# A two-layer decode kernel: the end of layer two rebuilt, one weight block fetched in row pairs, and a new order of loads and work

## The chip, the cores and the metric

The kernel runs on 1 core of one Trainium2 chip. The metric is the device time of one execution in microseconds (us); less is better. Profiles show one execution each, taken by the hardware profiler.

## What is computed

Four rows of 512 (one token each of four batches) pass an attention block and a gated block, twice, with the same weights and the same caches:

```python
def _A_ref(x, k_cache, v_cache, wq, wo):   # 32 query heads, 8 K/V heads of 128, 4096 positions
    q = (x @ wq), split into heads
    p = softmax(einsum(q, k) * Dh ** -0.5)
    return einsum(p, v), heads joined, @ wo
def _B_ref(x, w_gate, w_up, w_down):       # 512 -> 1792 -> 512
    return (sigmoid(x @ w_gate) * (x @ w_up)) @ w_down
x = x + _A_ref(_layernorm(x), k_cache, v_cache, wq, wo)
x = x + _B_ref(_layernorm(x), w_gate, w_up, w_down)
x = x + _A_ref(_layernorm(x), k_cache, v_cache, wq, wo)
x = x + _B_ref(_layernorm(x), w_gate, w_up, w_down)
```

## The kernel before

Attention is cut into 16 units, named by three digits: batch, half of the K/V heads (four heads, 16 query heads), layer. UNITS fixes their sequence; 301 is the last. A unit needs eight K tiles and eight V tiles of 512 KB (head s from 0 to 3, half q of the positions). They live in a ring of 24 slots. A tile of layer one that LOADS does not name again for layer two is kept in its slot until then: all of units 010, 110, 210 and 310, and two K tiles of 000. All weights have places of their own.

LOADS is the list of loads, issued by SP in this order. A word names kind, unit and piece: digits 0 to 3 are two single tiles, a to d both halves of one head as one DMA of 1 MB into two neighbouring slots, e to l one single tile. SP waits in order: a load whose slot is still in use holds all behind it. PAIRS names the blocks of w_o (eight heads, 1 MB each) that are fetched with two rows side by side, so that runs are twice as long; the merge of those heads then picks columns for even and odd rows apart.

A planner (`_Plan`) makes the program. Each operation is put with an engine, the keys that it reads and writes, an assumed cost and a rank, which comes from the place in LOADS of the data it needs, plus shifts (SHIFTS, by stage) and constants (CHAIN, PROJECT, KEPT_K and others). `schedule` replays all engines with assumed durations and takes the ready operation of least rank; this gives each engine's order, the slot of each tile, and fillers: constant matmuls (L1262) wherever PE would be idle. Some PSUM banks are locked by one user at a time (M, O, Q, P).

A unit runs as follows: DVE turns each K tile (L775); PE forms scores (L783), GROUPS[i] heads at a time; DVE and ACT form the exponentials (L807 to L842); PE multiplies with V (L874), two heads beside each other on column strips; ACT evicts (L903), PE merges into M (L916), DVE scales into oT (L938). The last unit's last pair of heads goes head by head, the second in bank G. `project` multiplies oT by a block of w_o into M (L1151) and adds it to x (L1162). In layer two it is called five times, the last two with four heads each. Then `last_chain` forms the row sums of x (L1183), the mean by a product with ones (L1187), x minus the mean twice (L1170, as fp32 xc and bf16 xT), squares (L1192), their sums (L1193), the mean square by small products (L1198), ACT's copy (L1203) and the power -1/2 on POOL (L1207). PE meanwhile runs gate and up products (L1027). The first up product in bank O waits for the power; ACT's sigmoid, DVE's product and transpose, w_down's products (L1098) and the output follow.

## Time and profile before

| | us |
|---|---|
| Median of 3 runs (lowest, highest) | 297.37 (297.33, 298.25) |
| The profiled execution | 298.3 |
| Its span, first to last instruction | 296.3 |
| Busy in the span: PE, DVE, ACT, POOL | 231.8, 171.0, 67.9, 10.9 |
| Mean granted TensorE clock | 0.983 of full |

In the page's rows L12 is line 12 of the program, PEld is PE's weight load, SPq the queue of the engine that issues the loads. Behind the bar of a group stand its busy time, the mean of one instruction in ns, and the idle time of the engine before them with what ended it. A row of a timeline begins with its start and its duration in us.

### The profile page before, as it was taken

The numbers are of one execution on the slowest core, as the hardware profiler recorded it, in microseconds if no ns is written. First come the engines' busy times: TensorE is split into PE (matmuls) and PEld (weight loads), VectorE is DVE, ScalarE is ACT, GpSimd is POOL, SyncE is SP. The second block draws the span as 40 slices with busy tenths as digits, with TensorE's granted clock in tenths as the row PEclk, the third lists the DMA queues.
The fourth block names the chain that finished last, engine by engine and source line by source line (L and its number), as shares of the span: only waits on it lengthen the run. The fifth ranks groups of instructions, "written<-read, shape, count | busy, mean of one in ns | idle before, by whom it ended". The sixth has DMA issues, their size and how long they took to land.

```text
span 296.3 us, 7884 instructions
## 1 busy us (share of the span) xinstructions
PE 231.8 (78%) x3440; PEld 112.4 (38%) x3440; DVE 171.0 (58%) x335; ACT 67.9 (23%) x179; POOL 10.9 (4%) x39
## 2 busy tenths in 40 slices
PE   1000684489988969998898889888997898997996
PEld 1000531144434424344464334454443354543443
DVE  4491277134351758995238878326889972388322
ACT  1000111110043210114442202323310234333512
POOL 7000000000000000000000000000000000000000
PEclk9999999779999989999999999999999999999999
DMA  7999999999999999999999999999999999999920
GB/s 279 428 424 421 421 395 395 422 420 390 390 418 374 369 421 409 413 410 420 404 385 410 411 412 416 408 401 357 385 414 409 409 408 407 406 405 410 406 106 3
DMA packets 28018, 114.03 MB, mean 385 GB/s; under 512 B 2768, under 2 KB 4816, under 8 KB 23504
## 3 DMA queue, kind: packets, MB, share of 16 engines
q1 hardware_dynamic: 27920, 113.52, 96.2%
q8 instruction: 27, 0.44, 0.6%
q14 instruction: 7, 0.06, 0.0%
q10 hardware_dynamic: 64, 0.01, 0.0%
HBM read 113.51 MB, written 0.00 MB: 383 GB/s over the span
## 4 chain that ended last, share of the span: by engine, by line
DMA 56%; PE 29%; DVE 7%; SPq 4%; issue 2%; ACT 1%; POOL 0%; ACTq 0%; DVEq 0%
DMA slots<-in_A_v_cache_dram 26%; DMA slots<-in_A_k_cache_dram 24%; PE S_ps L783 7%; PE PT_ps L1262 6%; DMA wd<-in_B_w_down_dram 6%; PE O_ps L874 5%; DVE slots L775 4%; SPq L581 4%; PE M_ps L963 2%; PE G_ps L1098 2%; PE G_ps L1027 1%; PE Q_ps L713 1%; PE U_ps L1027 1%; ACT pt_sb L842 1%; PE M_ps L916 1%
## 5 line engine op out<-in xcount | busy, mean ns | idle before, releaser
L775 DVE STREAM_TRANSPOSE slots<-slots 128x1024 int32<-128x1024 int32 x94 | 113.7, 1229 | 21.6 <-DMA slots<-in_A_k_cache_dram 20.4
L1262 PE MATMUL PT_ps<-wq 128*128 128x512 bf16 x308 | 82.9, 389 | 2.1 <-ACT pt_sb L842 2.1
L783 PE MATMUL S_ps<-slots,zq 128*32 128x512 bf16 x512 | 43.7, 406 | 7.2 <-DVE slots L775 3.4
L874 PE MATMUL O_ps<-slots,pt_sb 128*16 128x512 bf16 x504 | 37.9, 388 | 13.2 <-DMA slots<-in_A_v_cache_dram 7.7
L1262 PEld LDWEIGHTS PT_ps<-wq 128*128 128x128 bf16 x308 | 27.1, 100 | 34.6 <-issue 9.7
L783 PEld LDWEIGHTS S_ps<-slots,zq 128*32 128x32 bf16 x512 | 14.7, 97 | 27.5 <-DVE slots L775 8.6
L682 PE MATMUL Q_ps<-small,wq 128*128 128x4 bf16 x128 | 3.7, 166 | 24.6 <-DMA wq<-in_A_wq_dram 24.0
L903 ACT ACTIVATE slots<-O_ps 128x512 bf16<-128x512 f32 (+1 forms) x24 | 14.3, 595 | 37.2 <-PE O_ps L874 37.1
L821 ACT ACTIVATE p_sb<-S_ps,pt_sb 128x512 bf16<-128x512 f32 x16 | 13.3, 832 | 35.7 <-DVE pt_sb L814 31.5
L874 PEld LDWEIGHTS O_ps<-slots,pt_sb 128*16 128x16 bf16 x504 | 10.3, 88 | 28.0 <-issue 7.7
L842 ACT ACTIVATE pt_sb<-PT_ps 128x256 bf16<-128x256 f32 x32 | 10.8, 381 | 29.6 <-PE PT_ps L832 18.0
L963 PEld LDWEIGHTS M_ps<-oT,wo 128*128 128x128 bf16 x512 | 14.4, 96 | 6.1 <-DVE oT L942 1.7
L942 DVE TENSOR_TENSOR oT<-M_ps,real 64x8 bf16<-64x8 f32 x32 | 5.0, 155 | 20.2 <-PE M_ps L916 20.0
L963 PE MATMUL M_ps<-oT,wo 128*128 128x32 bf16 x512 | 15.8, 177 | 0.2
L748 DVE TENSOR_TENSOR zq<-Q_ps,real 128x256 bf16<-128x256 f32 x16 | 6.3, 395 | 16.3 <-ACT oT L692 10.5
L807 DVE TENSOR_REDUCE small<-S_ps 128x1 f32<-128x512 f32 x16 | 10.9, 683 | 5.8 <-PE S_ps L783 5.5
L1015 POOL TENSOR_TENSOR real<-real,small 128x1 f32<-128x1 f32 x8 | 4.4, 550 | 247.7 <-ACT real L1011 247.7
L682 PEld LDWEIGHTS Q_ps<-small,wq 128*128 128x128 bf16 x128 | 3.6, 104 | 24.8 <-DMA wq<-in_A_wq_dram 24.1
L916 PEld LDWEIGHTS M_ps<-small,slots 128*128 128x128 bf16 (+1 forms) x196 | 7.3, 107 | 11.8 <-ACT slots L903 6.1
L722 ACT ACTIVATE p_sb<-Q_ps 128x512 bf16<-128x512 f32 x8 | 4.8, 598 | 29.4 <-PE Q_ps L713 29.2
L916 PE MATMUL M_ps<-small,slots 128*64 128x4 bf16 (+2 forms) x196 | 9.5, 178 | 1.7 <-ACT slots L903 1.3
L713 PE MATMUL Q_ps<-wq,small 128*1 128x512 bf16 x128 | 9.8, 378 | 0.4 <-DVE small L989 0.3
(110 smaller groups left out, 174.5 us busy)
## 6 DMA issues: line engine op xcount, KB each, us to landing
slots<-in_A_k_cache_dram SPq DMA_DIRECT2D x66, 512.0 KB, 8.8
slots<-in_A_v_cache_dram SPq DMA_DIRECT2D x64, 512.0 KB, 10.4
slots<-in_A_v_cache_dram SPq DMA_DIRECT2D x16, 1024.0 KB, 14.9
slots<-in_A_k_cache_dram SPq DMA_DIRECT2D x14, 1024.0 KB, 13.5
wq<-in_A_wq_dram SPq DMA_DIRECT2D x2, 2048.0 KB, 17.6
wo<-in_A_wo_dram SPq DMA_DIRECT2D x4, 1024.0 KB, 16.8
wg<-in_B_w_gate_dram SPq DMA_DIRECT2D x1, 1792.0 KB, 16.8
wu<-in_B_w_up_dram SPq DMA_DIRECT2D x1, 1792.0 KB, 13.0
```

The source lines that it names most:

```text
L581: return e.dma_start(o, src)
L713: fns.append(lambda e, k=k, s=s: e.matmul(Q_ps[32 * s:32 * s + 1, :], lhsT=xT[:, b, k:k + 1], rhs=wq[:, k, hg * HC + s * 512:hg * HC + (s ...
L775: "dve", lambda e, t=t: e.transpose(ring[t.slot].bitcast(dt.int32), ring[t.slot].bitcast(dt.int32)),
L783: fns.append(lambda e, s=s, t=t, nn=nn, q=q: e.matmul(S_ps[qi][32 * s:32 * s + 32, :], lhsT=window(qi, s * NQ + nn, q), rhs=ring[t.slot].r ...
L807: dve(lambda e: e.tensor_reduce(ml[at], bank, AX.X, ALU.max, negate=True), [f"S{qi}s{s}" for s in ss], keys("ml", ss), 0.7)
L821: lambda e: e.activation(p_sb[at].rearrange("p (t j r) -> p t r j", j=32, r=2), bank.rearrange("p (t r j) -> p t r j", r=2, j=32), ACTF.Ex ...
L842: "act", lambda e, pr=pr: e.activation(pt_sb[:, (2 * i + pr) % 3], PT_ps[:, 256 * pr:256 * pr + 256], ACTF.Copy),
L874: fns.append(lambda e, m=m, at=at, v=v, c=c, q=q, pt=pt, o_ps=o_ps: e.matmul(o_ps[m:m + 16, :], lhsT=pt[:, at:at + 16], rhs=ring[v.slot][: ...
L903: lambda e, lent=lent, rows=rows, o_ps=o_ps, rows_of=rows_of: e.activation(ring[lent.slot][rows, 0:512], rows_of(o_ps[rows]), ACTF.Copy),
L916: return e.matmul(o, lhsT=turned[:, tt * P + at:tt * P + at + n], rhs=heads(tt), start=(tt == 0), stop=(tt == 3))
L963: fns.append(lambda e, k=k, n=n, h0=h0: e.matmul(M_ps[:, k * WIDE:(k + 1) * WIDE], lhsT=wo[:, h0 + n, k * P:(k + 1) * P], rhs=oT[:, b, h0 ...
L1262: S.filler(lambda e: e.matmul(PT_ps[:, 0:FILL], lhsT=wq[:, 0, 0:P], rhs=wq[:, 0, 0:FILL], start=True, stop=True), "PT")
```

## The change

The loads and the work are in a new order: LOADS, SHIFTS, GROUPS, LENT, the planner's constants and the assumed delays of loads are other values, and fillers are 256 columns wide, or 128 where 256 do not fit and no load is left to issue. Block 3 of w_o is fetched in row pairs too.

At layer two's end the last head's value products go in two parts, 288 columns to bank G and 224 to Q; ACT evicts the first and DVE the second. `last_part` takes the place of the last two `project` calls. The mean of x after the last block is not summed from x: the row sums of w_o's rows, made by DVE after the block's arrival and kept as two bf16 terms, are multiplied by oT onto the sum of the x before (`wo_mean`). The block's own product goes to bank S0, in two groups of four heads, and DVE forms `rest` (x minus mean) and then xc as one addition; ACT copies it to xT. The mean square is one product of ones by the squares and a masked sum on DVE (`bmask`) that also adds eps. The products of w_o are repeated over 64 columns instead of 32.

```diff
-DMA_DELAY = 0.979
-DMA_END = 1.047
-DMA_AGAIN = 2.392
+DMA_DELAY = 0.566
+DMA_END = 0.327
+DMA_AGAIN = 8.671
...
-PATIENCE = 2.164
+PATIENCE = 2.451
...
-LEAST = 4198
-WANTED = 35744
+LEAST = 13283
+WANTED = 154148
 FILL_FROM = 55.0
-FILL = 512
+FILL = 256
+SMALL = 128
+AMID = (2, 1)
...
-PAIRS = "02"
-GROUPS = "4244242442444444"
+PAIRS = "023"
+GROUPS = "2414222444442244"
...
-LENT = "K10021 V20001 V11100 V10130 V31101"
-CHAIN = 8.81
-PROJECT = 65.006
-KEPT_K = -26.257
-KEPT_V = 47.748
-REST_V = 60.815
...
-PUT_OFF = 69.06
+LENT = "V00020 V20001 K30001 V10101 V30110"
+CHAIN = 15.361
+PROJECT = -411.034
+KEPT_K = 2.445
+KEPT_V = 62.014
+REST_V = 286.312
...
+PUT_OFF = 365.25
 UNITS = "000 010 100 011 110 200 001 111 210 300 211 310 101 201 311 301"
-LOADS = "K010d wq1 K010a K000d K000c K000a V000c V000d wq0 V010b K000b K010b wo1 K100b K010c wg wo0 V000b V000a V010c K100a K1001 V010a wo2 V010d wo3 K1003 wu wd V1002 V1003 K2000 V100a K1103 K001l V100b K2001 K110b K110a K001g K1101 K2003 K2002 V110a K001k K001h K0012 V110b V1102 V1103 V200b V200a V0010 V0011 V2002 V2003 V001h K3001 K2103 V001l K3003 V001g K3000 K210a K2101 K210b V001k K3002 V210b V210a V2102 V2103 V3002 V3003 V3001 V3000 K3103 K201h K101f K101j K3101 K101h K101e K101i K1013 K201f K3100 K101g V3100 K3102 K2012 K201g K201e K201l K201k V3101 V101i V3103 V3102 V101e V101f V101j V1012 V101k V101l V201e V201i V201f K301l V201j K3011 K301e K301f K301i K301j V2012 K301k V2013 V301i V301f V301e V301j V301g V301k V301h V301l"
+LOADS = "V010b wq0 K100d K010a K000d wq1 V010d K0000 K0002 K000c K100c K010b K100b V0001 wo0 K100a wo1 K010c V010a V0000 K010d V010c wo2 wo3 V000c V000d wu wg wd V1002 V1003 K0013 K110b K2000 K110c K2002 V100a K110a V100b K2003 K110d K2001 K001i V110d V110b K001j K001h K001g V110a V110c V2000 V2001 V2002 V2003 V001j V001f V001e V001i K3000 K2101 V001k K210b V001l K300c K2103 K300d K210a V001h V001g K3002 V210a V210b V2102 V2103 V3002 V3003 V3000 V3001 K3103 K3101 K3100 K201k K101e V3101 K101h K101f K201g V3102 K3102 K101i K101g K201h K101j V3100 K2010 K1013 K201l V3103 K2012 V1010 V1011 V1012 V101k V101l K301j V201i V2010 V201j K301k K301f K301i K301h V2012 K301e K301g K301l V2013 V301a V301b V301g V301k V301h V301l"
...
+                if t + cost > at and not loads:
+                    op.fns, op.columns = [self.fill_small], 4 * SMALL
+                    cost = pe_cost(op, t)
...
+    FULL = 64
...
+    xc = spare[1][:, 0:16].rearrange("p (b k) -> p b k", b=B)
     sq = spare[0][:, 0:16].rearrange("p (b k) -> p b k", b=B)
-    xc = spare[1][:, 0:16].rearrange("p (b k) -> p b k", b=B)
+    rest = spare[0][:, 16:32].rearrange("p (b k) -> p b k", b=B)
+    bmask = spare[2][:, 0:B]
+    wo_mean = real[:, 68:76].bitcast(bf).rearrange("p (i n) -> p i n", i=2)
...
+    wo_sum = U_ps[:, FS:FS + 8]
...
-                                fns.append(lambda e, m=m, at=at, v=v, c=c, q=q, pt=pt, o_ps=o_ps: e.matmul(
-                                    o_ps[m:m + 16, :], lhsT=pt[:, at:at + 16], rhs=ring[v.slot][:, c * 512:(c + 1) * 512],
-                                    start=(q == 0 and c < 2), stop=(q == 1 and c >= 2),
-                                ))
+                                for bank, x0, x1 in ((G_ps, 0, 288), (Q_ps, 288, 512)) if alone else ((O_ps, 0, 512),):
+                                    fns.append(lambda e, m=m, at=at, v=v, c=c, q=q, pt=pt, bank=bank, x0=x0, x1=x1: e.matmul(
+                                        bank[m:m + 16, x0:x1], lhsT=pt[:, at:at + 16], rhs=ring[v.slot][:, c * 512 + x0:c * 512 + x1],
+                                        start=(q == 0 and c < 2), stop=(q == 1 and c >= 2),
+                                    ))
...
+                            "pe", fns, reads=[f"pt{part}", "Oz", "Gz", "Qz"], writes=["G", own("Q", first)] if alone else [own("O", first)],
+                            tiles=vs, rank=rank if len(some) == len(heads) else soon, columns=512 * 2 * len(vs), strips=2 * len(vs),
+                            lock=("Q" if alone else "O") if first else None,
...
+                cols = 288 if alone else 512
                 S.put(
                     "act",
...
+                    lambda e, lent=lent, rows=rows, o_ps=o_ps, rows_of=rows_of, cols=cols: e.activation(
+                        ring[lent.slot][rows, 0:cols], rows_of(o_ps[rows, 0:cols]), ACTF.Copy
...
-                    reads=["G" if alone else own("O")], writes=[lent.name], cost=0.6, rank=late, free=None if alone else "O",
+                    reads=["G" if alone else own("O")], writes=[lent.name], cost=0.17 + 0.43 * cols / 512, rank=late, free=None if alone else "O",
                 )
                 lent.users.append(S.ops[-1])
+                if alone:
+                    before = S.ops[-1].deps
+                    S.put(
+                        "dve",
+                        lambda e, lent=lent, rows=rows, cols=cols: e.tensor_copy(ring[lent.slot][rows, cols:512], Q_ps[rows, cols:512]),
+                        reads=[own("Q")], writes=["half"], cost=0.4, rank=late, free="Q",
+                    )
+                    for d in before:
+                        S._after(S.ops[-1], d)
+                    lent.users.append(S.ops[-1])
...
+                "pe", fns, reads=["sel_o"] + ([own("P")] if lent is None else ["half"] if alone else []), writes=[own("M", True)], cost=0.25, rank=late,
...
-            if k == 2:
+            if k == AMID[len(bs) > 1]:
                 amid()
...
+    def weight_sums(h0):
+
+        S.stage = "s"
+        for n in range(8):
+            S.put(
+                "dve", lambda e, n=n: e.tensor_reduce(wo_sum[:, n:n + 1], wo[:, h0 + n, :], AX.X, ALU.add),
+                reads=[f"wo{h0 // 8}"], writes=["U"], cost=0.6, rank=place[f"wo{h0 // 8}"] + 6.0,
+            )
+
+    def weight_means():
+
+        S.stage = "s"
+        rank = rank_v(seq[-1], 0)
+        S.put(
+            "dve", lambda e: e.tensor_scalar(wo_mean[:, 0], wo_sum, 1.0 / D, None, op0=ALU.mult),
+            reads=["U"], writes=["wo_mean0", "maskrs0", "maskrs1"], cost=0.16, rank=rank,
+        )
+        S.put(
+            "dve",
+            lambda e: e.scalar_tensor_tensor(
+                out=wo_mean[:, 1], in0=wo_sum, scalar=1.0 / D, in1=wo_mean[:, 0], op0=ALU.mult, op1=ALU.subtract
+            ),
+            reads=["U", "wo_mean0"], writes=["wo_mean1"], cost=0.16, rank=rank,
+        )
...
             cost=1.4, rank=-1e6,
         )
         S.put(
+            "dve", lambda e: e.tensor_reduce(bmask, ident.rearrange("p (m b) -> p b m", b=B), AX.X, ALU.add),
+            reads=["even"], writes=["pt2"], cost=0.3, rank=rank,
+        )
+        S.stage = f"z{h0}"
+        S.put(
             "dve", lambda e: e.tensor_reduce(xsum, x, AX.X, ALU.add),
             reads=[f"x{b}" for b in every_b], writes=[f"xsum{b}" for b in every_b], cost=0.2, rank=rank,
         )
         S.put(
-            "pe", lambda e: e.matmul(U_ps[:, 0:B], lhsT=ones, rhs=xsum, start=True, stop=True),
+            "pe", lambda e: e.matmul(U_ps[:, 0:B], lhsT=ones, rhs=xsum, start=True, stop=False),
             reads=["ones"] + [f"xsum{b}" for b in every_b], writes=["U"], cost=0.35, pairs=2, rank=rank,
         )
-        centre(xc, ["pt1"], rank)
-        centre(xT, [f"xT{b}" for b in every_b], rank)
-        S.put("dve", lambda e: e.tensor_tensor(sq, xc, xc, ALU.mult), reads=["pt1"], writes=["pt0"], cost=0.2, rank=rank)
-        S.put("dve", lambda e: e.tensor_reduce(xsq, sq, AX.X, ALU.add), reads=["pt0"], writes=[f"xsq{b}" for b in every_b], cost=0.2, rank=rank)
+        for g in range(2):
+            S.stage = f"z{h0 + 4 * g}"
+            heads = [f"oT{b}{h0 + 4 * g if (b, h0 // HG, 1) == seq[-1] else h0}" for b in every_b]
+            fns = []
+            for n in range(4 * g, 4 * g + 4):
+                for i in range(2):
+                    fns.append(lambda e, n=n, i=i: e.matmul(
+                        U_ps[:, 0:B], lhsT=wo_mean[:, i, n:n + 1].broadcast_to([P, P]), rhs=oT[:, :, h0 + n],
+                        start=False, stop=(n == 7 and i == 1),
+                    ))
+            S.put("pe", fns, reads=heads + ["wo_mean0", "wo_mean1"], writes=["U"], cost=0.0, rank=rank + 3.0 * g)
+            for k in range(KD):
+                fns = []
+                for n in range(4 * g, 4 * g + 4):
+                    fns.append(lambda e, k=k, n=n: e.matmul(
+                        S_ps[0][:, k * FULL:(k + 1) * FULL], lhsT=wo[:, h0 + n, k * P:(k + 1) * P],
+                        rhs=oT[:, :, h0 + n].unsqueeze(2).broadcast_to([P, B, FULL // B]),
+                        start=(n == 0 and k == 0), stop=(n == 7), skip_group_check=True,
+                    ))
+                S.put(
+                    "pe", fns, reads=heads + [f"wo{h0 // 8}"], writes=banks, rank=rank + 3.0 * g,
+                    columns=len(fns) * 4 * FULL,
+                )
+        rank = rank + 4.0
+        S.stage = "end"
+        S.put(
+            "dve", lambda e: e.tensor_tensor(rest, x, U_ps[:, 0:B].unsqueeze(2).broadcast_to([P, B, KD]), ALU.subtract),
+            reads=["U"] + [f"x{b}" for b in every_b], writes=["pt0"], cost=0.2, rank=rank,
+        )
+        moved = S_ps[0][:, 0:KD * FULL].rearrange("p (k b d) -> p b k d", k=KD, b=B)[:, :, :, 0]
+        S.put(
+            "dve", lambda e: e.tensor_tensor(xc, moved, rest, ALU.add), reads=banks + ["pt0"], writes=["pt1"], cost=0.2, rank=rank + 1.0,
+        )
+        S.put(
+            "act", lambda e: e.activation(xT, xc, ACTF.Copy),
+            reads=["pt1"], writes=[f"xT{b}" for b in every_b], cost=0.2, rank=rank + 1.0,
+        )
+        S.put(
+            "dve", lambda e: e.tensor_tensor(x, moved, x, ALU.add),
+            reads=banks + [f"x{b}" for b in every_b], writes=[f"x{b}" for b in every_b], cost=0.2, rank=rank + 9.0,
+        )
+
+    def last_chain(rank):
+
+        S.stage = "end"
+
+        S.put("dve", lambda e: e.tensor_tensor(sq, xc, xc, ALU.mult), reads=["pt1"], writes=["sq"], cost=0.2, rank=rank)
 
         def spread():
-            fns = []
-            for c in range(4):
-                fns.append(lambda e, c=c: e.matmul(Q_ps[32 * c:32 * c + B, 200:201], lhsT=xsq, rhs=mean1, start=True, stop=True))
             S.put(
-                "pe", fns, reads=["ones", "Qz"] + [f"xsq{b}" for b in every_b], writes=[own("Q", True)], cost=0.25, rank=rank, pairs=8, lock="Q",
+                "pe", lambda e: e.matmul(Q_ps[:, 200:216], lhsT=ones, rhs=spare[0][:, 0:16], start=True, stop=True),
+                reads=["ones", "Qz", "sq"], writes=[own("Q", True)], cost=0.3, rank=rank, pairs=2, lock="Q",
             )
             S.put(
-                "act", lambda e: e.activation(var[:, 0:1], Q_ps[:, 200:201], ACTF.Copy, bias=eps),
-                reads=[own("Q")], writes=["junk"], cost=0.2, rank=rank, free="Q",
+                "dve",
+                lambda e: e.scalar_tensor_tensor(
+                    out=sq, in0=Q_ps[:, 200:216].rearrange("p (b k) -> p b k", b=B), scalar=eps / KD,
+                    in1=bmask.unsqueeze(2).broadcast_to([P, B, KD]), op0=ALU.add, op1=ALU.mult, accum_out=var[:, 0:1],
+                ),
+                reads=[own("Q"), "pt2"], writes=["junk", "sq"], cost=0.27, rank=rank, free="Q",
             )
             S.put(
                 "pool", lambda e: e.tensor_tensor(rs_row, var[:, 0:1], mhalf, ALU.pow),
@@ -1240,6 +1332,8 @@
     passed = []
     first_q(0)
     queries(0, 0.0)
+    late = seq[-1][1] * HG
+    weight_sums(late + 8)
     for i, (b, hg, l) in enumerate(seq):
         passed.append(seq[i])
         if i == 1:
@@ -1252,14 +1346,20 @@
         if i and seq[i - 1][1:] == (1, 0):
             assert b != seq[i - 1][0]
...
-    late = seq[-1][1] * HG
-    for h0 in (HG - late, HG - late + 8, late, late + 8, late + 12):
+    weight_means()
+    for h0 in (HG - late, HG - late + 8, late, late + 8):
         rank = max(rank_v((b, h0 // HG, 1), h0 // 8 % 2) for b in every_b)
-        project(h0, rank + (PROJECT if h0 // HG != seq[-1][1] else 1.0), 8 if h0 < late + 8 or h0 >= late + HG else 4)
-    last_chain(rank_v(seq[-1], 1) + 3.0)
+        if h0 == late + 8:
+            last_part(h0, rank + 1.0)
+        else:
+            project(h0, rank + (PROJECT if h0 // HG != seq[-1][1] else 1.0))
+    last_chain(rank_v(seq[-1], 1) + 6.0)
...
-    S.filler(lambda e: e.matmul(PT_ps[:, 0:FILL], lhsT=wq[:, 0, 0:P], rhs=wq[:, 0, 0:FILL], start=True, stop=True), "PT")
+    def constant(n):
+        return lambda e: e.matmul(PT_ps[:, 0:n], lhsT=wq[:, 0, 0:P], rhs=wq[:, 0, 0:n], start=True, stop=True)
+
+    S.filler(constant(FILL), constant(SMALL), "PT")
```

28 lines of the change are left out of this document (10 added, 18 removed).

## The prediction

> **What bounds the kernel now.** I read the page first, then the load queue's waits, then busy time by stretches of 5 us, then the last 12 us instruction by instruction.
>
> ```profile
> span 296.3 us, 7884 instructions
> GB/s 279 428 424 421 421 395 395 422 420 390 390 418 374 369 421 409 413 410 420 404 385 410 411 412 416 408 401 357 385 414 409 409 408 407 406 405 410 406 106 3
> DMA 56%; PE 29%; DVE 7%; SPq 4%; issue 2%; ACT 1%; POOL 0%; ACTq 0%; DVEq 0%
> ```
>
> The loads run at 400 GB/s or a little more from the second of 40 slices to the last but two. The kernel is therefore two things in a row: a stream of 113.5 MB, and a tail that can begin only when its last piece has landed. PE's 29% of the chain is mostly work beside which the stream goes on. Four kinds of stretch show what the stream could still save or lose:
>
> ```profile
> 20.00:25.00 5.00, 0.00 (x0) 0.00 (x0) 3.05 (x3) 0.00 (x0) 0.00 (x0) 1.00 1.01 421
> 35.00:40.00 5.00, 4.38 (x78) 2.31 (x77) 3.93 (x4) 0.45 (x1) 0.00 (x0) 1.00 1.03 377
> 55.00:60.00 5.00, 2.86 (x14) 0.81 (x16) 0.00 (x0) 0.00 (x0) 0.00 (x0) 0.74 1.01 423
> 70.00:75.00 5.00, 4.87 (x75) 2.27 (x71) 0.49 (x3) 0.60 (x1) 0.00 (x0) 1.00 1.04 385
> 95.00:100.00 5.00, 4.84 (x63) 2.28 (x64) 4.34 (x9) 1.12 (x3) 0.00 (x0) 1.00 0.94 310
> 150.00:155.00 5.00, 4.90 (x107) 3.01 (x103) 0.95 (x6) 2.10 (x7) 0.55 (x1) 1.00 0.96 371
> 200.00:205.00 5.00, 4.56 (x72) 2.15 (x68) 2.53 (x5) 2.07 (x9) 0.55 (x1) 1.00 0.99 379
> 205.00:210.00 5.00, 4.37 (x78) 2.17 (x78) 4.92 (x8) 0.61 (x5) 0.00 (x0) 1.00 0.97 345
> 230.00:235.00 5.00, 4.68 (x59) 1.99 (x52) 4.45 (x5) 0.78 (x2) 0.00 (x0) 1.00 1.03 411
> ```
>
> The last columns are the granted clock, the DMA share and GB/s. 421 is a stretch of 1 MB loads and 411 one of 512 KB loads, both with a full queue. Between 95 and 100, 150 and 155, and 200 and 210 us the rate falls without a weight in transit. Against 411 GB/s these four rows are short of 101, 40, 32 and 66 GB/s for 5 us each, which is 1.23 + 0.49 + 0.39 + 0.80 = 2.9 us of lost stream. Their neighbours are a little low too, so I call the loss 2.9 to 3.5 us.
>
> ```profile
> SPq L382 <- PE S_ps L783: 61.7, 14, 8.8
> SPq L581 <- PE G_ps L1027: 10.2, 1, 10.2
> ```
>
> These are waits of the queue that issues the loads: reason, sum, count, longest. A load needs free slots of the ring, and a slot becomes free when the last matmul on its tile is done. Most of this waiting costs nothing since earlier loads are still under way. It costs when it outlasts them, as the 10.2 us wait (which ended at 195.8 us) did: the low rows at 200 to 210 us follow it.
>
> **The change part by part.**
>
> *w_o's block 3 in row pairs.* In the order of before, block 1, which is fetched singly, is the 1 MB up to 15.7 MB of the list. At 0.42 MB per us with 2 us of start it lands near 39 us, in the row of 377 GB/s. Block 3 ends at 30.2 MB, near 74 us, in the row of 385 GB/s. Against 411 these rows lose 0.41 and 0.32 us. Pairing removes the short rows of block 3. I take 0.4 us, and 0 to 0.5 as bounds. The evictions of that group of heads must now reorder columns and the merge has three small products instead of one; they lie beside the stream and cost nothing as long as the ring has free slots.
>
> *More 1 MB loads.* Counted in the two lists: 113.51 MB in both, with 30 double loads before and 34 after. At 421 instead of 411 GB/s a MB takes 2.49 instead of 2.55 us, so four of them save 0.24 us (bounds 0 and 0.35). No unit reads more or less than before.
>
> *The order of loads and of all work* (the list, the shifts, the constants) is new as a whole, and this term decides the sign. Bytes and ring are the same, so the order can move only the lost 2.9 to 3.5 us. What can be read off: in both lists w_down ends 34.87 MB of weights and first units, and until then the 16 tiles of unit 010 stay in the ring for unit 011. So the tight place near 95 us remains: eight free slots must cover w_down's landing, its products, the queries and the scores of 011. What differs is that w_q is complete after 8.4 MB instead of 11.5, so that the first scores start some 7 us earlier, and the scores of unit 100 go tile by tile. Both free slots sooner. Bounds: all of the loss gone, -3.5 us; or the loss doubled, +3.5 us. With the first place remaining and the other two open I take a gain of 1.2 us, about a third of the loss.
>
> *The end of layer two.* The last load and what follows it:
>
> ```profile
> 270.05 0.33 SPq L581 DMA_DIRECT2D slots<-in_A_v_cache_dram  x1
> ...
> 284.94 0.60 PE L874 MATMUL G_ps<-slots,pt_sb 128*16 128x512 bf16 x4
> ...
> 285.59 0.59 ACT L903 ACTIVATE slots<-G_ps 64x512 bf16<-64x512 f32 x1 [1.57 <-PE G_ps L874]
> ...
> 286.15 0.17 DVE L1162 TENSOR_TENSOR real<-M_ps,real 128x16 f32<-128x16 f32 x1 [0.94 <-PE M_ps L1151]
> ...
> 286.47 0.25 PE L916 MATMUL M_ps<-small,slots 128*128 128x32 bf16 x4 [0.20 <-DVE real L1162]
> ...
> 286.76 0.16 DVE L938 TENSOR_TENSOR oT<-M_ps,real 128x4 bf16<-128x4 f32 x1 [0.43 <-PE M_ps L916]
> ...
> 286.98 0.56 PE L1151 MATMUL M_ps<-oT,wo 128*128 128x32 bf16 x16
> ...
> 287.65 0.17 DVE L1162 TENSOR_TENSOR real<-M_ps,real 128x16 f32<-128x16 f32 x1 [0.73 <-PE M_ps L1151]
> 287.86 0.17 DVE L1183 TENSOR_REDUCE real<-real 128x4 f32<-128x16 f32 x1
> 288.08 0.38 PE L1187 MATMUL U_ps<-real 128*128 128x4 f32 x2
> ...
> 288.57 0.17 DVE L1170 TENSOR_TENSOR pt_sb<-real,U_ps 128x16 f32<-128x16 f32 x1 [0.55 <-PE U_ps L1187]
> 288.66 0.16 DVE L1170 TENSOR_TENSOR small<-real,U_ps 128x16 bf16<-128x16 f32 x1
> 288.78 0.17 DVE L1192 TENSOR_TENSOR pt_sb<-pt_sb 128x16 f32<-128x16 f32 x1
> 288.88 0.74 PE L1027 MATMUL G_ps<-wg,small 128*4 128x448 bf16 x12
> 288.99 0.17 DVE L1193 TENSOR_REDUCE real<-pt_sb 128x4 f32<-128x16 f32 x1
> ...
> 289.45 0.20 PE L1198 MATMUL Q_ps<-real 128*4 128x1 f32 x8
> ...
> 289.80 0.17 ACT L1203 ACTIVATE real<-Q_ps 128x1 f32<-128x1 f32 x1 [3.62 <-PE Q_ps L1198]
> 290.05 0.55 POOL L1207 TENSOR_TENSOR real<-real,small 128x1 f32<-128x1 f32 x1 [29.92 <-ACT real L1203]
> ...
> 290.65 0.72 PE L1027 MATMUL O_ps<-wu,small 128*4 128x320 bf16 x16 [0.18 <-POOL real L1207]
> ```
>
> ```profile
> slots<-in_A_v_cache_dram SPq DMA_DIRECT2D x1, 512.0 KB, 14.7
> ```
>
> The last load lands 14.7 us after its issue at 270.05, at 284.75, and its matmuls start at 284.94. For the operations that before lacks I use these groups (mean ns is the last number ahead of the second bar):
>
> ```profile
> L807 DVE TENSOR_REDUCE small<-S_ps 128x1 f32<-128x512 f32 x16 | 10.9, 683 | 5.8 <-PE S_ps L783 5.5
> L1068 DVE SCALAR_TENSOR_TENSOR p_sb<-slots,real,O_ps 128x192 bf16<-128x192 f32 x1 | 0.4, 373 | 0.0
> L1132 DVE SCALAR_TENSOR_TENSOR real<-G_ps,real 128x4 f32<-128x4 f32 x4 | 0.9, 222 | 5.7 <-PE G_ps L1098 5.7
> L1132 DVE DVE_READ_ACCUMULATOR real<-G_ps,real 128x1 f32 x4 | 0.3, 84 | 0.0
> L1262 PE MATMUL PT_ps<-wq 128*128 128x512 bf16 x308 | 82.9, 389 | 2.1 <-ACT pt_sb L842 2.1
> ```
>
> The eviction is cut at column 288 and shared: ACT's part, on the line between 0.17 us (L1203, one column) and 0.59 (512), takes 0.41; DVE's 224 columns take about 0.4 (L1068, 192 columns: 0.37). The merge before was held until 286.47 by the projection's addition into x (286.15 to 286.32), which frees M. After, that projection goes to another bank, so the merge starts 0.10 behind the copies, at 286.10, and the last oT ends at 286.55 instead of 286.92. Against that, the first group's 24 products (8 for the mean, 16 for w_o, at 0.56/16 = 0.035 us each 0.84 us) start behind the last value matmuls and can hold the merge for up to 0.22 us; I count 0.1. The second group's 24 products then run from 286.7 to 287.55. Addition, sum, mean matmul and their handovers (287.65 to 288.57) go: x minus the mean is formed beside the products, and one addition from 287.66 to 287.83 gives xc. It ended at 288.74 before, so 0.91 us are won here. ACT's copy for xT adds a step of some 0.25, so the gate starts at 288.14 instead of 288.88.
>
> Variance: the square ends at 288.04. One fp32 product takes the place of reduction and eight small ones; with handovers it is 0.5 (288.03 to 288.57 around L1187), and it may stand behind the gate's first four matmuls, 0.25 at most, of which I count 0.2. The masked sum on DVE takes 0.31 (0.22 + 0.08, L1132) in place of ACT's copy. So the power starts at 289.13 instead of 290.05, and O's products at 289.73 instead of 290.65. What follows is unchanged. The tail gains 0.9 us; bounds 1.2 (nothing held) and 0 (merge and fp32 product held in full, 0.17; the masked sum as slow as L1068, 0.15; the eight split matmuls 0.5 above the 0.60 of four).
>
> The split turns four value matmuls of 512 columns into eight, and each pair of two strips goes out as strip a, a, b, b. The matmuls of before go a, b, a, b; I take it that halves overlap as wholes do and the time stays 0.60. [...]
>
> *What is hidden.* Eight row sums of w_o on DVE at 0.68 (L807's 512 columns) are 5.5 us, placed some us behind block 1's arrival. Between 55 and 60 us DVE does nothing; without that cover each would delay one transpose by 0.7. Mean weights, mask and the 64 column products lie ahead of the last load, and fillers of 256 instead of 512 columns only take time in which PE had nothing to do. 64 columns need no more than 32 as long as 0.035 us per product is set by the weight load. I count 0 for all of these.
>
> **Sum.** -0.4 - 0.24 - 1.2 - 0.9 = -2.75 us. The profiled execution took 298.3 us with its span of 296.3, so it would take 295.6. It lies 0.9 us above the median of the runs, 297.37, to which the same difference gives 294.6.
>
> **Rivals.**
> 1. *The ring no longer starves.* All 2.9 us come back: -0.4 - 0.24 - 2.9 - 0.9 gives 292.9. For it: the earlier w_q, the finer scores. Against it: the place near 95 us stays.
> 2. *Pairs hold the queue* (slower). A double load waits for two neighbouring free slots and holds everything behind it on SP. Between 35 and 55 MB the new list has ten double loads of K and V where the old has six: among them all of unit 110's, which stay in the ring as unit 010's leave it, while unit 011 is on its way. If that doubles the loss, +3.5 - 1.55 gives 299.3. It decides the sign from a loss of 3.5 + 1.55, some 5 us, on. Against it: the SP queue's long waits of before were mostly covered.
> 3. *Order and end cancel out.* An order about 1 us worse and a tail held on PE (gain 0.4): +1.0 - 0.64 - 0.4, 297.3, no difference. Against it: the steps removed from the tail were all on the chain.
>
> **How the numbers follow.** 0.3% is 0.9 us here, about what a measurement tells from no change. My case has 0.45, with its own range of 293.3 to 296.2. Rival 1 has 0.16, rival 3 0.14 and rival 2 0.25, since a wholly new order is the one term that the old trace bounds on both sides only. Faster is the first two, 0.61; same 0.14; slower 0.25. For 8 in 10 the range runs from 292.4, which takes in rival 1, to 299.4, which takes in about half of rival 2.
>
> **What would show it.** In the stretches of 5 us after: rates of 400 or more outside the weights, and the place near 95 us still low. From the last value matmuls to O's products: 4.8 us instead of 5.7, with the merge less than 0.15 behind the copies. A power that starts later than 4.6 us behind those matmuls would refute the tail's sum. More than 5 us lost below 411 GB/s would make the prediction wrong.

## The result and the profile after

| | us |
|---|---|
| Before, median of 17 runs beside it (lowest, highest) | 297.45 (297.14, 300.75) |
| After, median of 17 runs (lowest, highest) | 300.73 (298.29, 303.85) |
| Ratio after to before, 95% interval | 1.0077 (1.0051 to 1.0103) |
| The profiled execution after, its span | 298.65, 296.7 |

The changed kernel is about 0.8% slower: 294.6 was predicted, and the median lies beyond the upper end of the range, 299.4. Its executions spread over 5.6 us where most of before's lie within 1, and the profiled one, 298.65, is one of the shortest. It shows what the change does when all goes well; what goes wrong in most executions is seen in profiles of the same kernel that were taken later (below). Single times here are medians of all runs, while the ratios leave disturbed runs out (in e21 two of six, of 339 and 373 us), so the two can differ a little.

The page of the profiled execution after: span, PE's and PE's weight loads' busy time with the number of instructions, and the instruction queue (packets, MB, share of the DMA engines).

```profile
span 296.7 us, 8528 instructions
PE 238.9 (81%) x3759; PEld 140.0 (47%) x3759; DVE 177.9 (60%) x355; ACT 68.1 (23%) x179; POOL 10.9 (4%) x39
q8 instruction: 29, 0.48, 0.6%
```

Each matrix product has its weight load, 3,759 of each and 7,518 instructions of TensorE in all. The queue q8 has 29 packets of 0.48/29 MB, some 16 KB or 260 of these instructions each; before it has 27 packets for 6,880, some 255 each. That q8 brings TensorE's program is read from this match (the other instruction queue, q14, has 6 packets). This row of the page of before was not read for the prediction.

Busy time by stretches, after, in the columns that the prediction used (granted clock, DMA share and GB/s last):

```profile
70.00:75.00 5.00, 4.39 (x68) 2.39 (x68) 0.60 (x4) 1.68 (x4) 0.00 (x0) 1.00 0.99 407
75.00:80.00 5.00, 4.13 (x99) 2.83 (x100) 1.46 (x7) 1.86 (x5) 0.00 (x0) 1.00 1.03 407
...
90.00:95.00 5.00, 4.90 (x83) 2.47 (x80) 0.46 (x3) 2.11 (x9) 0.55 (x1) 1.00 1.00 379
95.00:100.00 5.00, 4.85 (x67) 3.16 (x66) 4.83 (x9) 1.49 (x4) 0.00 (x0) 1.00 0.95 387
205.00:210.00 5.00, 4.79 (x69) 2.58 (x68) 4.90 (x9) 0.98 (x3) 0.00 (x0) 1.00 0.99 365
210.00:215.00 5.00, 4.89 (x88) 2.79 (x89) 4.16 (x8) 2.12 (x6) 0.00 (x0) 1.00 0.98 347
250.00:255.00 5.00, 4.94 (x82) 2.83 (x82) 1.75 (x6) 2.21 (x6) 0.55 (x1) 1.00 1.04 374
255.00:260.00 5.00, 4.25 (x80) 2.48 (x76) 1.67 (x5) 1.35 (x6) 0.28 (x1) 1.00 0.95 360
280.00:285.00 5.00, 4.47 (x84) 2.47 (x84) 1.12 (x6) 3.23 (x6) 0.00 (x0) 1.00 0.68 270
```

The same view of before, in stretches that the prediction did not show:

```profile
75.00:80.00 5.00, 4.77 (x65) 2.31 (x66) 1.16 (x4) 0.60 (x1) 0.00 (x0) 1.00 1.05 394
...
250.00:255.00 5.00, 4.94 (x84) 2.27 (x83) 1.37 (x5) 2.83 (x10) 0.55 (x1) 1.00 1.04 412
255.00:260.00 5.00, 4.62 (x95) 2.78 (x94) 2.13 (x9) 1.82 (x7) 0.42 (x1) 1.00 1.01 400
280.00:285.00 5.00, 4.88 (x90) 2.64 (x84) 0.68 (x4) 1.64 (x4) 0.00 (x0) 1.00 0.70 276
```

In this execution the place near 95 us has improved (387 against 310), 70 to 80 us is faster (other loads stand there now), 205 to 215 us is low as 200 to 210 us was (365 and 347 against 379 and 345), and a new low place has come at 250 to 260 us. Over all 52 stretches from 20 to 280 us, what is missing to 411 GB/s adds up to 5.7 us after and to 5.7 us before: in this execution the order has moved the loss and not lowered it.

The last load after, its issue and its time to landing:

```profile
274.30 0.33 SPq L591 DMA_DIRECT2D slots<-in_A_v_cache_dram  x1
...
slots<-in_A_v_cache_dram SPq DMA_DIRECT2D x1, 512.0 KB, 11.3
```

By the trace it lands at 285.65, and before's at 284.79: the loads end 0.86 us later, though this is one of the shortest executions.

The end of layer two, after, in the order of time:

```profile
284.40 1.11 PE L1173 MATMUL M_ps<-oT,wo 128*128 128x64 bf16 x32
...
285.44 0.30 PE L885 MATMUL G_ps<-slots,pt_sb 128*16 128x288 bf16 x2
...
286.18 0.29 PE L885 MATMUL G_ps<-slots,pt_sb 128*16 128x288 bf16 x2
...
286.84 0.41 ACT L915 ACTIVATE slots<-G_ps 64x288 bf16<-64x288 f32 x1 [1.73 <-PE Q_ps L885]
286.84 0.40 DVE L925 CAST slots<-Q_ps 64x224 bf16<-64x224 f32 x1 [0.39 <-PE Q_ps L885]
...
287.38 0.25 PE L938 MATMUL M_ps<-small,slots 128*128 128x32 bf16 x4
...
290.42 0.55 POOL L1299 TENSOR_TENSOR real<-real,small 128x1 f32<-128x1 f32 x1 [30.15 <-DVE pt_sb L1292]
...
291.03 0.72 PE L1049 MATMUL O_ps<-wu,small 128*4 128x320 bf16 x16
```

From the last value matmuls (286.18) to O's products (291.03) are 4.85 us, where before had 5.71 (284.94 to 290.65). But these matmuls start 1.24 us later than before's. Of that, 0.86 us is the later landing. The other 0.38 is TensorE's, which had no pause there: the projection of 1.11 us at 284.40 stood ahead of the value matmuls at 285.44, and these ahead of the last. From the last landing to O's products are 5.38 us, where before had 5.86. So here the end gains 0.48 us and the stream loses 0.86, which together is the 0.4 us by which the span is longer.

### The profile page after: what moved, and what is told of

Same layout as the page of the kernel before. It is cut to its first block, busy times and chain, and to the rows that moved or that the text cites. A ratio compares the mean times of both kernels' runs of the same rounds, so it can differ in the third digit from the quotient of the medians.

```text
span 296.7 us, 8528 instructions
## 1 busy us (share of the span) xinstructions
PE 238.9 (81%) x3759; PEld 140.0 (47%) x3759; DVE 177.9 (60%) x355; ACT 68.1 (23%) x179; POOL 10.9 (4%) x39
## 4 chain that ended last, share of the span: by engine, by line
DMA 58%; PE 28%; DVE 5%; SPq 4%; issue 2%; ACT 1%; DVEq 0%; ACTq 0%
DMA slots<-in_A_k_cache_dram 30%; DMA slots<-in_A_v_cache_dram 28%; PE S_ps L793 9%; PE O_ps L885 6%; SPq L591 4%; PE PT_ps L1360 4%; DVE slots L785 4%; PE Q_ps L723 1%; PE M_ps L985 1%; PE G_ps L1120 1%; PE M_ps L1173 1%; PE G_ps L1049 1%; PE M_ps L938 1%; PE U_ps L1049 1%; PE PT_ps L842 1%
## 5 line engine op out<-in xcount | busy, mean ns | idle before, releaser
L1360 PE MATMUL PT_ps<-wq 128*128 128x256 bf16 x545 | 75.2, 276 | 0.0
L793 PE MATMUL S_ps<-slots,zq 128*32 128x512 bf16 x512 | 57.3, 410 | 16.0 <-DVE slots L785 13.5
L1360 PEld LDWEIGHTS PT_ps<-wq 128*128 128x128 bf16 x545 | 48.2, 100 | 19.2 <-issue 13.4
L885 PE MATMUL O_ps<-slots,pt_sb 128*16 128x512 bf16 x504 | 37.1, 380 | 8.8 <-DMA slots<-in_A_v_cache_dram 5.4
L793 PEld LDWEIGHTS S_ps<-slots,zq 128*32 128x32 bf16 x512 | 18.4, 98 | 42.4 <-DVE slots L785 20.7
L964 DVE TENSOR_TENSOR oT<-M_ps,real 64x8 bf16<-64x8 f32 x48 | 7.5, 156 | 13.8 <-PE M_ps L938 13.5
L938 PE MATMUL M_ps<-small,slots 128*64 128x4 bf16 (+2 forms) x228 | 10.1, 175 | 2.6 <-DVE real L997 1.0
L938 PEld LDWEIGHTS M_ps<-small,slots 128*64 128x64 bf16 (+1 forms) x228 | 7.7, 104 | 8.7 <-issue 3.2
```

The lines of the kernel that those rows point to most:

```text
L793: fns.append(lambda e, s=s, t=t, nn=nn, q=q: e.matmul(S_ps[qi][32 * s:32 * s + 32, :], lhsT=window(qi, s * NQ + nn, q), rhs=ring[t.slot].r ...
L885: fns.append(lambda e, m=m, at=at, v=v, c=c, q=q, pt=pt, bank=bank, x0=x0, x1=x1: e.matmul(bank[m:m + 16, x0:x1], lhsT=pt[:, at:at + 16], ...
L938: return e.matmul(o, lhsT=turned[:, tt * P + at:tt * P + at + n], rhs=heads(tt), start=(tt == 0), stop=(tt == 3))
L1360: return lambda e: e.matmul(PT_ps[:, 0:n], lhsT=wq[:, 0, 0:P], rhs=wq[:, 0, 0:n], start=True, stop=True)
```

## The experiments

Every run has runs of the kernel before beside it on the same chip; ratios are to those. The chips differ a little: before took 297.6 us in the first group of runs, 298.9 in the second, 298.0, 297.7 and 297.6 in the last three.

### Which part: the end, or the order

The changed code with the old order (e1), the old code with the new order (e2), and the changed kernel as it is (e3).

```diff
 e1, against after:
-LOADS, SHIFTS, PAIRS, GROUPS, LENT and the constants of after
+those of before; FILL = SMALL = 512
 e2, against before:
-LOADS, SHIFTS, PAIRS, GROUPS, LENT, the constants and FILL of before
+those of after
```

> The new end and its helpers with the loads, shifts, pairs, constants and 512-column fillers of before. If the new order is what costs (theory), the end's gain stands alone: 296.4 to 297.0 us, some 0.5 to 0.9 under before, with before's small spread (1 to 1.5 us). If the end itself costs (rival: its row sums or its PE work delay the ring), 298 to 300 us.

> The old end with the new loads, shifts, pairs, constants and 256-column fillers. If the new order or its fillers cost (theory), 300.5 to 302 us: as slow as the whole change plus the 0.9 us that the old end lacks, with the same spread of 3 us or more. If the end is what costs (rival), 296 to 297.5 us.

> The changed kernel unaltered, for a second profile and its spread. Theory: median 299.5 to 301 us, spread 3 us or more, and in a slower execution the loads fall below 400 GB/s in places where the profile of after does not. Rival (the first set of runs was disturbed): 298 to 298.7 us with a spread of 1 us.

The end alone: 297.72 us, 1.001 (0.9985 to 1.0035). The order alone: 301.8, 1.0116 (1.0074 to 1.0158). Both together: 299.99, 1.0039 (1.0007 to 1.0071). So the order costs, 3.4 us by its ratio, and the end does not cost, but does not bring 0.9 us either. Why not stands in the timeline of TensorE in e1:

```profile
284.44 0.37 PE L1243 MATMUL U_ps<-oT,real 128*128 128x4 bf16 x8
284.66 0.63 PE L1251 MATMUL S_ps<-oT,wo 128*128 128x64 bf16 x16
285.22 0.30 PE L885 MATMUL G_ps<-slots,pt_sb 128*16 128x288 bf16 x2
```

The first group's 24 products stand ahead of the last value matmuls, not behind them. These start 1.40 us behind the last landing (283.82), where before's start 0.15 behind it, and from that landing to O's products are 6.20 us. Run e7 puts them behind, by a false dependency, and changes nothing else:

```diff
 e7, against e1:
-reads=heads + ["wo_mean0", "wo_mean1"]
+reads=heads + ["wo_mean0", "wo_mean1", "G"]
-reads=heads + [f"wo{h0 // 8}"]
+reads=heads + [f"wo{h0 // 8}", "G"]
```

> The new end with before's order (as in the run of the end alone), but the first group of four heads' 24 products stands behind the last value matmuls on PE instead of ahead of them; all else is the same. If those 24 products, and not the new end's own steps, hold the last value matmuls 1.6 us behind the last landing (theory), 296.4 to 296.9 us, about 1 us under the end alone. If the end gains nothing in itself (rival), 297.5 to 297.9 us.

297.7 us, 0.997 (0.994 to 1.000): better than e1 by about 0.4%, on another chip and with overlapping intervals. In its profile the last value matmuls start 0.66 us behind the landing, and from the landing to O's products are 5.50 us, 0.70 less than in e1.

### Fillers, delays, the projection's rank, the list

> The changed kernel with fillers of 512 columns as before; the orders of loads, DVE, ACT and POOL are the same as in the changed kernel. If the narrow fillers let the clock drop and so cause the loss and the spread (first form of the theory), 297 to 298 us, a mean clock of 0.98 in each run and a spread under 1.5 us. If the loads' order does it whatever the fillers (second form), 299.5 to 301 us and the same spread.

Fillers of 512 columns (FILL = SMALL = 512, with the loads and the other engines' work in the same order): 299.42, 1.0028 (0.9998 to 1.0058). The narrower fillers are not the cause.

> The changed kernel planned with before's assumed delays of loads (0.979, 1.047 and 2.392 in place of 0.566, 0.327 and 8.671). The orders of loads, DVE, ACT and POOL stay as in the changed kernel; PE gets more fillers ahead of its waits and a few groups swap. If PE waits without fillers, because the plan expects data too early, and loses its clock there (theory), 298 to 299 us and a mean clock of 0.98 or more. If the order of loads and work itself starves the ring (rival), 299.5 to 300.5 us as the changed kernel.

With the old DMA_DELAY, DMA_END and DMA_AGAIN, which change nearly only the fillers' number and places: 298.71, 0.9966 (0.9927 to 1.0005). The low place at 250 to 260 us is gone in its profile:

```profile
250.00:255.00 5.00, 4.95 (x100) 3.31 (x97) 2.48 (x5) 1.67 (x4) 0.55 (x1) 1.00 1.03 407
255.00:260.00 5.00, 4.67 (x64) 2.23 (x66) 1.03 (x6) 1.99 (x9) 0.55 (x1) 1.00 1.03 406
```

That is (407 - 374 + 406 - 360) x 5 / 410 = 0.96 us, but it is one profile, and the fillers matter in another way too, as the next runs show: e5 shares what they find.

> The changed kernel with PROJECT 0 instead of -411: only the last 25 us differ, where the projections of layer two's first blocks no longer stand ahead of unit 201's value matmuls and of the last unit's. If they hold the last unit's exponentials (which wait for those value matmuls to release a buffer) and so the last value matmuls, 1.1 us behind the last landing (theory), 298.8 to 299.3 us, some 1 us under the changed kernel. If the landing sets that place anyway (rival), 299.8 to 300.3 us.

PROJECT = 0.0 in place of -411.034, which alters only the last 25 us: 299.78, 1.001 (0.9972 to 1.0048). The last value matmuls still start late, at 285.22. A miss: the backlog on TensorE is not the rank's alone.

> The kernel before with the new list of loads alone; shifts, groups, pairs, constants and fillers are before's, so that ranks no longer fit the list as they were tuned to. If the list is what starves the ring (theory), 300 us or more. If it is the ranks and groups around it (rival), 298 to 299.5 us, above before because of the misfit.

The new list with the old ranks and shifts: 315.08, 1.053. List and ranks belong together, and this tells nothing of the list as such.

### What makes most executions of the new order long

Profiles of long executions show a drop of TensorE's granted clock to 0.50 and starved loads behind it (in e21 0.50 from 84 to 88 us, and 242 GB/s from 95 to 100 us). Three runs test whether a wait of TensorE sets this off, with the changed kernel beside them (e17).

```diff
 after the plan is made:
+    for target, late in HOLES.items():
+        by[target].deps.add(by[late])
+    for target, (source, times) in PLUGS.items():
+        at = S.prog["pe"].index(by[target])
+        ...
+            S.prog["pe"].insert(at, op)
 e14: 55 more fillers at ten waits; e15: HOLES = {797: 125}; e16: the same and 13 fillers there
```

> The changed kernel, unaltered, as the measure for the three runs beside it. Both theories: about 1.004 to 1.008 of the kernel before, with executions in two groups some 2.7 us apart.

> The changed kernel with 55 more throwaway products of TensorE at ten places where its traces show TensorE waiting 0.3 to 1.7 us with nothing to do; every order of work and loads is the same. Theory A (the two groups come from spells of half TensorE clock that a long wait without products sets off, and each costs the loads some 2 us): the upper group gets thinner or goes, so the median falls by 1 to 2.5 us against the changed kernel run beside it, and the mean granted clock of the executions rises. Rival B (the groups come from elsewhere, from the chip's memory for instance, and the clock is only a companion): no change beyond 0.3%, or a loss of up to 0.5 us, as the added products delay work where a wait would have ended sooner.

> The changed kernel with one wait made longer by about 1.3 us: the value products near 190 us (for which TensorE waits 0.76 us in the shown profile) also wait for the next load, so TensorE stands still some 2.1 us. Theory A: the granted clock falls to 0.50 within 3 us of it, the loads of 195 to 205 us fall below 350 GB/s, and the executions come out 1.5 to 2.5 us longer, hardly any in the lower group. Rival B: at most the 1.3 us that the products come later, more likely 0 to 0.5 us, since later products wait less.

> As the run with the longer wait at 190 us, but with 13 throwaway products of 256 columns ahead of it (about 1.8 us), so that TensorE works through it. Both the wait and the order are those of that run, only the clock should differ. Theory A: no fall of the clock at 190 us, loads of 195 to 205 us at 380 to 410 GB/s, and the time of the unaltered changed kernel within 0.6 us. Rival C (what costs is that the products and the buffers they free come later): as slow as the run with the bare longer wait.

After again: 301.45, 1.0083 (1.0052 to 1.0114). With 55 fillers: 298.56, 1.0008 (0.9974 to 1.0041), 2.9 us less. With the longer wait 302.29, 1.0144 (1.0101 to 1.0188); with that wait filled 301.66, 1.0118 (1.0082 to 1.0154). These two intervals overlap, and both lie little above the kernel beside them (0.8 us for the bare wait, where theory A asked 1.5 to 2.5), so the times do not tell theory A from rival C. The profiles do, as far as one each goes; the wait of the first came out at 1.69 us. Stretches of the run with the bare wait, then of the run with the filled one:

```profile
196.00:198.00 2.00, 1.92 (x26) 1.26 (x26) 0.00 (x0) 0.60 (x1) 0.00 (x0) 0.77 1.03 412
198.00:200.00 2.00, 2.00 (x42) 1.67 (x40) 0.33 (x2) 0.00 (x0) 0.00 (x0) 0.50 0.99 387
200.00:202.00 2.00, 2.00 (x27) 0.98 (x25) 0.41 (x3) 0.56 (x3) 0.00 (x0) 0.88 0.43 172
```

```profile
196.00:198.00 2.00, 2.00 (x45) 1.50 (x46) 0.40 (x4) 0.00 (x0) 0.00 (x0) 1.00 1.02 408
198.00:200.00 2.00, 2.00 (x38) 0.87 (x38) 0.23 (x1) 0.73 (x4) 0.23 (x1) 1.00 0.94 371
200.00:202.00 2.00, 1.94 (x33) 0.97 (x26) 0.93 (x3) 1.39 (x3) 0.32 (x1) 1.00 1.01 391
```

Without the fillers the clock falls to 0.50 and the loads to 172 GB/s; with them it stays at 1.00. But all three long profiles here (e15, e16, e17) share something earlier, at 82 us, that the 55 fillers moved by accident. So the 55 were split: the first 8, which stand ahead of it (e18), and the other 47 (e19). Another kernel moves 8 fillers from 56 us to just ahead of it (e20), and the changed kernel ran again (e21).

```diff
 e18: PLUGS = {254: (1340, 8)}
 e19: PLUGS = the other nine places of e14
 e20: fillers 1333 to 1340 dropped, PLUGS = {329: (1385, 8)}
```

> The changed kernel, unaltered, as the measure for the three runs beside it: most executions at 300 to 302 us, a few at 296.5 to 298.5.

> The changed kernel with only the first 8 of the 55 throwaway products (ahead of the value products near 60 us, where TensorE waits for a load anyway). They move by 8 products the place in TensorE's program at which a 16 KB packet of the instruction queue must have landed. Theory F (in most executions TensorE stands 2.1 us near 82 us, in the middle of the third of three projections in a row, since that packet starts 1.8 us late; this sets off the half clock and the starved loads of 90 to 100 us): with the place moved the stop is shorter, most of the 2.9 us of the run with all 55 products is here too, and the time lies 1.5 to 3 us below the unaltered kernel. Theory A (the long waits elsewhere set off the half clock): at most a third of it, under 1 us.

> The changed kernel with the other 47 throwaway products at the nine later waits, from 108 us on; the program up to 105 us is untouched. Theory F: the stop near 82 us stays in most executions, the profile shows it or not as the packet starts late or not, and the time is within 1 us of the unaltered kernel. Theory A: 2 to 3 us below it.

> The changed kernel with 8 of its 12 throwaway products of 56 us moved ahead of the third projection near 80.7 us. The count of instructions up to the stop is the same, so the 16 KB packet is wanted at the same product, but TensorE comes there some 1.1 us later. Theory F: the stop shrinks by about 1.1 us in every execution (from 2.1 to 1.0 us where the packet is late, to nothing where it is not), the clock stays up more often, and the time lies 1 to 2.5 us below the unaltered kernel. Theory A: no gain, or 0 to 0.5 us lost for work that comes 1.1 us later at a tight place.

| | us | ratio (95%) |
|---|---|---|
| e21, after again | 301.4 | 1.0107 (1.0062 to 1.0152) |
| e18, 8 fillers early | 298.51 | 1.0011 (0.9974 to 1.0047) |
| e19, the other 47 | 300.28 | 1.0067 (1.0034 to 1.0099) |
| e20, 8 fillers moved | 298.91 | 1.0013 (0.9978 to 1.0047) |

The 8 bring 2.9 us, as much as all 55 did, the 47 some 1.1 us with overlapping intervals (theory F allowed 1, theory A asked 2 to 3), and moving 8 brings 2.5 without adding an instruction. This fits theory F and not theory A. TensorE's timeline after (first two rows, the short execution) and in e21 (the last two, a long one); the bracket is the idle time ahead of the row and what ended it, and "issue" is nothing that the profile shows:

```profile
80.73 0.89 PE L985 MATMUL M_ps<-oT,wo 128*128 128x32 bf16 x29
82.09 0.23 PE L985 MATMUL M_ps<-oT,wo 128*128 128x32 bf16 x3 [0.47 <-issue]
```

```profile
80.85 0.89 PE L985 MATMUL M_ps<-oT,wo 128*128 128x32 bf16 x29
83.89 0.24 PE L985 MATMUL M_ps<-oT,wo 128*128 128x32 bf16 x3 [2.15 <-issue]
```

TensorE stops after product 29 of the 32 of one projection, 0.47 us after and 2.15 in e21, and waits for no data that the profile shows: the first 29 used the same tiles. The instruction queue has one packet in the stretch from 79 to 81 us after, and the same row from 81 to 83 us in e21, whose stretch from 79 to 81 has none:

```profile
q8 instruction: 1, 0.02, 3.4%
```

By the trace's packet records it runs from 79.52 to 80.60 after and from 81.46 to 82.56 in e21, 1.9 us later. TensorE goes on 1.3 to 1.5 us behind its end in both, and so it does in e18, e20 and e22 (1.3 to 1.6). That it waits for the packet is inferred from this; no view names what it waits for. The same product stood 0.76 us in e3 and 0.17 in e8, whose profiled spans are 295.2 and 295.7, and 2.14 to 2.15 in e15, e16, e17, e19 and e21, with spans of 298.6 to 302.8. The order alone, e2, has it too, 2.10. In e18, with 8 products more ahead of it, the place has moved by 8, from product 29 to product 21; in e20 it has not moved, but TensorE comes there later:

```profile
81.86 0.43 PE L985 MATMUL M_ps<-oT,wo 128*128 128x32 bf16 x11 [0.38 <-issue]
```

```profile
83.56 0.23 PE L985 MATMUL M_ps<-oT,wo 128*128 128x32 bf16 x3 [1.32 <-issue]
```

What follows the long stop, in e21 by stretches:

```profile
80.00:85.00 5.00, 2.85 (x62) 2.23 (x57) 0.33 (x3) 0.40 (x2) 0.00 (x0) 0.76 1.07 432
85.00:90.00 5.00, 5.00 (x44) 2.30 (x44) 0.49 (x2) 1.07 (x5) 0.55 (x1) 0.56 0.97 396
90.00:95.00 5.00, 4.95 (x89) 4.05 (x91) 1.88 (x7) 0.75 (x4) 0.00 (x0) 1.00 0.81 307
95.00:100.00 5.00, 4.85 (x82) 2.14 (x78) 2.01 (x4) 2.60 (x9) 0.55 (x1) 1.00 0.67 242
```

The clock is 0.50 from 84 to 88 us and 1.00 from 90 us on, eight products of w_up or w_gate take up to 0.96 us where they took 0.55, w_down's products start at 92.14 instead of 89.10, and the load queue's longest wait between 78 and 102 us, which ends with them, grows by 2.9 us (first after, then in e21):

```profile
SPq L387 <- PE G_ps L1120: 12.5, 1, 12.5
```

```profile
SPq L387 <- PE G_ps L1120: 15.4, 1, 15.4
```

The loads then lack (379 - 307 + 387 - 242) x 5 / 410 = 2.6 us against the short execution, and the last load lands at 288.05, 2.4 us later.

In e5, too, the place has moved to product 21, and the stop is 0.37 us.

The stop at 82 us is not the only thing that makes executions long. The profile of e18, a long one, has it at 0.38 us but has a second stop, at 184 to 186 us (timeline). Behind it the clock falls and then the loads (stretches):

```profile
186.01 1.40 PE L885 MATMUL O_ps<-slots,pt_sb 128*16 128x512 bf16 x16 [1.76 <-issue]
```

```profile
186.00:190.00 4.00, 3.99 (x50) 1.54 (x51) 1.00 (x4) 1.49 (x3) 0.00 (x0) 0.57 1.03 410
190.00:195.00 5.00, 5.00 (x91) 3.45 (x92) 0.94 (x5) 1.25 (x3) 0.00 (x0) 0.66 1.03 410
195.00:200.00 5.00, 5.00 (x89) 2.71 (x85) 1.02 (x5) 1.83 (x7) 0.55 (x1) 1.00 0.84 309
```

The profile of e4 has no stop at 82 us and a span of 297.3: there TensorE waits 1.72 us for a load ahead of 191.6 us, and the granted clock is 0.50 from 192 to 194 us.

Two last kernels keep the shift at 82 us and take it back before 186 us (8 fillers left out between 101 and 175 us), the second with the 21 late fillers of e14 besides.

> The changed kernel with the 8 throwaway products ahead of the value products near 60 us, and 8 others left out one by one between 101 and 175 us, so that TensorE's program is shifted by 8 products at 82 us (as in e18_shift) and not shifted near 186 us, where the profile of e18_shift shows a second stop for instructions, of 1.76 us, and the half clock after it. Theory F: neither stop is over 0.5 us in most executions; the time is 0.5 to 1.5 us below that of e18_shift against the same measure, so 0.994 to 0.999 of the kernel before, and most executions lie at 296.5 to 298. If the packets come late by chance and not by place, it is that of e18_shift, about 1.001.

> As e22_both_places, and the throwaway products of the four waits from 217 us on (21 products), which cover TensorE's waits of 0.7 to 1.1 us there. Theory F alone: the time of e22_both_places, within 0.5 us. If the waits late in the kernel also let the clock fall now and then (the 1.1 us of e19_other_plugs), 0.3 to 1 us below it.

299.84, 1.0015 (0.9975 to 1.0054), and 298.93, 1.0019 (0.9988 to 1.0049). The stop at 186 us is 0.32 us in both profiles, but at 82 us the packet came late after all, with 2.29 us in e22:

```profile
83.54 0.46 PE L985 MATMUL M_ps<-oT,wo 128*128 128x32 bf16 x11 [2.29 <-issue]
```

In e23 it is 0.94. So both missed what theory F gave them (0.994 to 0.999), and e22's median is no better than e3's 299.99 on the same chip. The shift makes long executions rarer but does not end them: of 47 executions of the unaltered changed kernel 8 took less than 299 us, of 60 of e14, e18, e20, e22 and e23 31 did. These sets ran at different times and not all on one chip, and how often the packet itself was late is known only from one profile each. No version was shown to beat the kernel before. Nearest are e5 and e7, whose intervals just reach 1.0005 and 1.000.

## Why the prediction was wrong

*The step that failed* is "The order of loads and of all work", taken as a gain of 1.2 us "with the first place remaining and the other two open"; the order alone costs 3.4 us. The prediction looked at the order only as a matter of bytes and free slots. Even by that measure nothing was won in the shown execution: the place near 95 us has 387 GB/s instead of 310, but other places lost as much, and the last load lands 0.86 us later, where pairs, double loads and order were to bring it 1.84 us earlier. (In e3, the shortest profile of the same kernel, it lands at 284.17, 0.6 us earlier.) The loss of 2.9 to 3.5 us, of which a third was to be won, was taken from four rows; all rows of before give 5.7. So its sign of being wrong, more than 5 us lost below 411 GB/s, holds for the kernel before as well and tells nothing.

What it left out is that a new order is also a new program for TensorE, which is what most of the long profiles show: the stop of 1.3 to 2.3 us, the granted clock of 0.50 and, in e21, some 2.6 us less stream behind it. Before, one projection (line 963) at this time is followed by fillers:

```profile
77.95 0.95 PE L963 MATMUL M_ps<-oT,wo 128*128 128x32 bf16 x32
...
79.48 2.10 PE L1262 MATMUL PT_ps<-wq 128*128 128x512 bf16 x9
```

That is 64 instructions in 0.95 us and then 18 in 2.1. After, three projections (78.07, 79.44 and 80.73) take 192 instructions in some 4 us, and the stop stands in the third, just ahead of w_gate, w_up and w_down, on which the queue's longest wait hangs. For the old order the packets could be counted in the page and the instructions in the timeline. For the new one the instructions follow from the plan. That a packet would come late could not be read from either.

*Row pairs, -0.4.* Of the right size, but not measured apart. The sum's own row gives 0.32 us. By the trace block 3 lands at 77.8 us before, in rows of 385 and 394 GB/s, and at 70.7 us after, in rows of 404 and 405 (60 to 70 us); against 411 that is (26 + 17 - 7 - 6) x 5 / 411 = 0.36 us. But the loads beside the block are others too. *Four more double loads, -0.24:* not measured apart.

*The end, -0.9.* Right in its steps and too large in what it brings, 0.48 us from the landing to O's products. The copies took 0.41 and 0.40 as worked out; the merge follows 0.13 us behind them; the power starts 4.24 us behind the last value matmuls (4.19 by the sum, 4.6 would have refuted it); 4.85 us to O's products against 4.8. But the sum took the start of the value matmuls as given, 0.19 us behind the last load; it was 0.53 after and 1.40 in e1. In e1 the first group's products come ahead of the last value matmuls, where the prediction had them behind and counted 0.1 for what they hold up; in the changed kernel the projection of 1.11 us at 284.40 does the same. The 64 columns, counted as 0, cost a little: 16 products take 0.63 us instead of 0.56. A tail is only as early as the engine that begins it.

*The split matmuls.* The eight halves (286.18 to the copies at 286.84) take 0.66 us, before's four wholes 0.65 (284.94 to 285.59). By the timeline both strips' first halves start at 286.18 and both second halves at 286.31, so no second half held back the other strip's first.

*The rivals.* Rival 2, slower at 299.3, had the sign and over half of the size (1.9 of 3.3 us), but not the mechanism. The load that waited 12.5 or 15.4 us on w_down's products is the second part of K0013, a single load of 512 KB into a slot that layer one's end still works in; the first double load, K110b, stands behind it in the list. Rival 3 had both signs, a worse order and a tail held on TensorE, but 1 us for the order where e2 has 3.4. Rival 1 (292.9) and the forecast needed a stream that no execution had: the shortest of all runs of the new order, 296.27 us in e22, is some 1.4 us below that run's median of before (297.64).

*What stays open.* Why the stop is 2.10 to 2.15 us in some executions (six of the nine profiles whose program is the same up to there; in e21 the packet starts 1.9 us later) and 0.17 to 0.76 in the others. Its place in the program is the same, TensorE's timeline from 76 us up to it is the same but for 0.3 us, and the weights beside it land within 0.5 us of each other. A spell of half clock (rows of 0.50) between 61 and 69 us stands ahead of the stop of 2.15 us in e21 and of the one of 0.76 in e3. What makes the other long executions long, such as e4's and e18's, was seen in one profile each. How much the low place at 250 to 260 us costs over many executions was not measured.

## What to carry to other kernels

Here 8 products more ahead of the stop moved it by 8 (e18), and it stood where 192 instructions took some 4 us; look for such places of many short products in a row, above all ahead of work that frees a buffer; fillers ahead of such a place helped here (e20, by its median). When executions of one kernel spread by more than the gain in question, profile several: the one shown first was a good one. A gain at the end counts only if the engine that starts the end is free when the last byte lands (its products started 0.53 us behind the landing after, and 1.40 in e1).
